# Sliding-window attention and a gated FFN on one core: loads ordered closer to the scores, early scores in separate banks, new engine orders

## The chip, the cores and the metric

The kernel runs on one core of a Trainium2 chip. The metric is the device time of one execution in microseconds, the median of several runs; less is better. A core has TensorE (matmul; the profile lists its weight loads as PEld), VectorE (DVE), ScalarE (ACT), GpSimd (POOL) and SyncE (SP). Each works through its own list of instructions in order. Here POOL and SP mostly issue DMA transfers, which 16 DMA engines carry out.

## The reference

Four sequences, eight heads, 768 positions, head dimension 64. Each query sees the last 128 positions and the four first ones (the sinks); the result goes through RMS normalisation and a gated FFN.

```python
scores = scale * np.matmul(q, k.transpose(0, 1, 3, 2))
keep = (pos[None, :] < 4) | ((rel >= 0) & (rel < 128))
a = softmax(np.where(keep, scores, -1e9))
x = np.matmul(a, v)                       # to [3072, 512]
xn = x / np.sqrt(np.mean(x * x, axis=-1, keepdims=True) + 1e-06) * rms_g
g = xn @ w_gate                           # 512 x 1536
out = (g * sigmoid(g) * (xn @ w_val)) @ w_out
```

## The kernel before

**Blocks.** The 3072 rows are 24 blocks g of 128 (six per sequence, or batch, b). In this text q5, k5, v5 are the loads of block 5, qT5 and kT5 the transposed tiles.

**Attention of a block.** POOL loads q, k and v, cast to bf16 by the DMA (L353, L357); block 0's q and k come through SP in float32 and are cast on an engine (L349). For blocks 0 to 7 q and k are transposed on TensorE (L445) and copied to the tile `qkT` by DVE or ACT (L452); from block 8 on SP does it with DMA transposes (L459). Scores are kept transposed: keys of block g against the queries of g (the own part) and of g+1 (the next part). Blocks 0 and 1 have their mask added by a matmul (L467) and no mask product. Blocks 2, 3, 6, 12 and 18 do whole scores (L485) and a mask product on DVE (L547); the others do only the needed triangles (L563, or L501 for the last of a batch), masked on DVE (L584) or from block 16 on POOL (L597, L526). ACT takes the exponentials (L536, L572, L512). AV (L616, L621) sums e times v, with a column of ones in the v tile giving the denominators. Those ones are written by DVE, one memset for each batch (L278). Sinks have their own small scores (L742), exponentials (L751) and AV (L606, L641); their v rows come by four SP loads into `vsink`, which DVE first clears (L326), and DVE makes `vsk` of them (L734). DVE divides (L660, L661), called n below; ACT squares (L669); DVE does the rest of the normalisation in eight small steps (L676 to L693), called the x chain. The gain `gb` is a product of TensorE, scaled by ACT (L428, L431). x is transposed on TensorE (L708) and copied (L714) for blocks 0 to 7, by SP's DMA transposes (L720) after that.

**FFN.** Six groups of four blocks. For a chunk of columns, g and v matmuls (L975), tanh on ACT (L982), two DVE steps (L988, L998), and the output matmuls (L1008), copied out by ACT (L1016) and stored by SP. Group 0 goes in four chunks of 128 columns, groups 1 and 2 in two of 256.

**Order.** Every step is entered with `op` in a fixed sequence, and so has a number. `ORDER` lists for each engine the numbers in the order in which the engine gets them, `TURNS` interleaves the engines, and `BANKS` gives each PSUM tile one of eight banks. What a step "needs" is only checked against these lists; the waits in the program come from the data: tiles read, written or reused, and banks taken again. `LOAD_LEAD`, `LEAD_FROM`, `GATE_FROM` and the priorities were used to make the lists and enter the program through them alone. Fifty-six small matmuls on zeros (`warm`, L421) stand in TensorE's list as fillers, all of them before 22 us.

A bank holds 512 float32 for each partition. The scores of a whole block take four, two heads with own and next part side by side in each:

```python
out=BANK[slot][:, j * 256 + n0 * P:j * 256 + n1 * P],
lhsT=qkT[pr, 1, hp, t * P:(t + 1) * P],
rhs=qkT[pr, 0, hp, (t + n0) * P:(t + n1) * P],
```

The first loads in POOL's list are q1, ident (make the identity), bias (make the mask), k1, v0, wg 0-1, q2, q3, v1, k2. In SP's list the stages of k0 and q0 come first, then the gain row and the sink rows.

Of the kernel before, what the change touches and what calls it, by code (L numbers as in the profile page):

```python
# [89 lines left out]
""",  # L90
    "ACT": """
24 20 22 199 177 175 178 176 182 180 181 183 168 188 222 204-206 211 207 212 209 191 210
217 226 228 227 229 195 598 220 236 603 613 618 608 243 633 628 260 623 245 247 246 248
638 278 262 255 264-267 197 280 282 284 653 273 320 648 643 295 297 659 290 322 299 301
300 302 276 324 325 293 326 327 309 664 678 669 683 674 333 312 693 340 316 341 688 342
343 698 355-357 336 358 703 370 371 708 372 318 373 349 385 364 387 718 713 723 739 379
399 401 400 402 728 418 419 733 420 393 421 409 763 758 778 768 754 773 744 749 427 433
414 783 434-436 448 449 793 450 798 451 442 808 788 819 803 463-466 813 457 824 480 475
482 494 496 497 495 513 488 514 515 504 834 838 516 848 843 853 829 863 868 858 878 873
525 883 531-533 893 509 888 534 899 923 549-551 928 552 938 543 567-569 918 570 585 587  # L100
933 943 948 561 953 579 958 909 904 968 593 963 914 973 1008 1003 994 998 1013 1028 1023
989 1038 1018 1033 984 1053 1048 1043 979 1069 1059 1064 1072 1073
""",
    "DVE": """
# [13 lines left out]
""",  # L118
    "POOL": """
25 8 9 26-28 31 34 30 32 37 35 29 38 33 39 41 42 40 43 45 47 44 48 46 49 36 50 53 57 52  # L120
54 51 56 63 62 60 55 58 64 61 59 65-99 467 469 468 470 481 100 483 101-108 517 520 109
518 519 535 538 537 536 110 553 555 554 571 573 556 572 588 586 574
""",
    "SP": """
# [7 lines left out]
ASDDSDGDPDPSPDPPPPPGPPPGPDPGPPDDPGAGPPPPADGPPPPGPPSPDPSADPGSDPSPGAAAPAGPAPPDAPPGPPAPDPAP  # L132
PPPADPGPDAGPPDPPDGAPPGPAPPAGDPAPAPDGADAPDGPAPPPADPAGPDAPADAGPPPPAPADGAPADGPPPPPAPPDPGPPD
DPAGPDPAGPDPGAPDDGPDGPDADGDPDGPADADPGAADPGPGDPADGAPDPGADAPGADADPGDPAPPDAPPDADAPGDPPADAGP
AAGPAPDAPPDPADPDAPGDAPDDGDPAPGDPPGSAAPGADAPGDPDGPPPDAGDAPGDADPPGADPAGDSAPPAGASPADPADSADP
PPGADAPGPSADDPGASAPGDPGSAPPGDPSADGAPDASDAPPDADPAGPPSAAADPAADPADPDAPAGADPGADPPDAPPADDPDGS
PDAPASAGDPPAPAGDSPADAPADDPPAGSADPPDASDPAGPADPSDDPGAPDDPADAPDGSDPDGPAGAPADSAPPADSDPPDGPDS
PDAGASPAAPDASGDPADSPDSDPGSPPPDDPSDGPDADPAPADPSDPSPDPSPDDAPDPDAPADPADAPDADAPDPDPASAPDASAP
DSADPADPDPASAPASADPAPPDASDPDAPSDASPADPDADPDPDPDAPASAPPDASADPAGPDGPGDPDGAPDPDPDPDAPAAGPSA
DGPAASGPADSPAGDPPGDDPGPPDGPDAAGPPDAGADPAGPAAGDPADAGPGPDSPGDPDASGPDGAADSPDAPDSDPPDSPDAPDS  # L140
ADPDSAPPDSDPSDAPDASPADDPDPDPADAPAAPDASADPADSPGSDGPDGSPGPGPAPAPADPAPDADPADAPDAGAPDGPGPAAP
AAPPADGDPPDGPDGDGPPAAPDSPGDPGAGPDAPPDPDPDPDAADPADPDDPAPAADPSDPDPDDPAAPPSPDDPAAPDPPSPPDPA
PSDSDSPASDPDPPPAAPDDPDPDPPAAPSDPDPAPDDPDPPPPAAPDADPSDPAAPDPDPAAPDDPDPDAPADPDPDPDPPDPAAPD
SPSDPPPPPAAPSASSPAADS
"""
BANKS = """
0123456701234567012345645645635654353513714370432704614654154761061305147237235720165760
7615743764051726351402376152376015237653746573746574631547613547647136210735462047136524
7012473650241762350741602735410721356421305406354063420675134632745013274350174362507431
6542371607152374153275461237104573604156324175032407615342047562310462317460170414217326  # L150
5047314243270172316412040572153042573045
# [4 lines left out]
def kernel(  # L156
# [40 lines left out]
    LOADS = "q-1 k-1 v-0 w-0-2 v-1 qkv-2 qkv-3 w-2-4 w-4-6 w-6-8 w-8-9 w-9-10 w-10-12 qkv-4 wo-0-6 qkv-5 wo-6-12 qkv-6 qkv-8 qkv-7"  # L197
    LOADS += "".join(f" qkv-{g}" for g in range(9, NB))
# [6 lines left out]
    GATE_FROM = 8  # L205
    LOAD_LEAD = 10
    LEAD_FROM = 10
# [146 lines left out]

    def load_v(g):
        b, t = divmod(g, NT)
        nc.gpsimd.dma_start(out=V16[b][:, t, :, 0:D], in_=block_of(v, g))  # L357
# [26 lines left out]
    def sw_block(g, what="qkv"):  # L384
        for n in what:
            needs = [("s", g - LOAD_LEAD)] if g >= LEAD_FROM else []
            if n == "v":
                sw_load(lambda g=g: load_v(g), [("v", g)], 860,
                        needs=needs + [("vone", g // NT)])
            else:  # L390
                src = q if n == "q" else k
# [57 lines left out]

    def copy_t(n, g, eng):  # L450
# [13 lines left out]
    def mask_bias(g):  # L464
        for u in range(2):
            for hi in range(2):
                nc.tensor.matmul(  # L467
                    out=bank(("s", g, u, hi)), lhsT=ident if g % NT else idnos,
                    rhs=bias.rearrange("p n c -> p (n c)").unsqueeze(1).to_broadcast(
                        (P, 2, 2 * P)),  # L470
                    start=True, stop=False, skip_group_check=True,
                )

    def scores(g, n0, n1):
        b, t = divmod(g, NT)
        qkT = T["qkT", b]
        for u in range(2):
            for j in range(2):
                hp = 2 * u + j
                for hi in range(2):  # L480
                    pr = slice(hi * D, (hi + 1) * D)
                    slot = ("s", g, u, hi)
                    if slot not in BANK:
                        bank(slot)
# [656 lines left out]
```

## Time and profile before

| | |
|---|---|
| median of 3 runs | 241.71 us (241.56 to 242.35) |
| span of the profiled execution | 241.9 us |
| TensorE / DVE / ACT / POOL busy | 231.3 / 187.4 / 122.8 / 89.2 us |
| FFN first stage on TensorE (L975) | 143.5 us |
| output matmuls (L1008) | 65.3 us |
| last matmul group's evacuation starts | 238.97 us |
| POOL loads q, k, v, 128 KB each | 8.1, 9.6, 8.9 us from issue to landing, median |
| DMA transposes to `qkT` | 7.7 (q) and 9.0 us (k) |

The page cuts the span into 40 slices of 6.05 us; a digit is the busy share in tenths. TensorE's busy time overlaps, since a matmul's latency counts though the next one has started; the distance from start to start is the better price. Lines of a timeline give the start, the time until the last of the merged instructions ends, engine, line, operation and tile, and in brackets the idle time before and what ended it. A chain of waits is followed back from the last instruction to what released it.

### The profile page before, as it was taken

The page shows a single profiled execution, that of the slowest core. Times are in us where ns is not written, and L with a number is a line of the kernel's source. Part 1 is how long each engine was busy: PE and PEld are TensorE (multiplying, and loading weights), DVE is VectorE, ACT ScalarE, POOL GpSimd, SP SyncE. Part 2 cuts the span into 40 slices and gives each one's busy share as a digit, 9 for nine tenths or more (in the row PEclk, how much of TensorE's full clock was granted, in tenths as well). Part 3 has the DMA queues.
Part 4 walks back from the last instruction along what each step waited for, and adds up shares of the span by engine and source line. Part 5 has one row for each costly group of instructions (what it writes and reads, how often), then busy time and mean ns, then how long its engine had stood idle before and what let it go on. Part 6 is the DMA issues. An engine that isn't in the chain of part 4 may idle for free.

```text
span 241.9 us, 5897 instructions
## 1 busy us (share of the span) xinstructions
PE 231.3 (96%) x2329; PEld 147.6 (61%) x2354; DVE 187.4 (77%) x478; ACT 122.8 (51%) x267; POOL 89.2 (37%) x116
## 2 busy tenths in 40 slices
PE   7889999999879999999999999999999999999995
PEld 5568986876668776777876644445554444444443
DVE  3599989989979999999898989994569946537520
ACT  4776368667766574337654464454543321233112
POOL 8985894597526554000004982022540000000000
PEclk9999999999999999999999999999999999999999
DMA  9999999999999999999601999527010114101024
GB/s 128 143 183 195 182 178 194 162 143 139 137 151 152 138 143 154 132 233 156 126 2 24 119 150 123 131 70 128 3 23 0 32 36 173 43 0 47 0 87 173
DMA packets 113741, 27.42 MB, mean 113 GB/s; under 512 B 103857, under 2 KB 110769, under 8 KB 113714
## 3 DMA queue, kind: packets, MB, share of 16 engines
q0 software_dynamic: 81760, 13.90, 79.3%
q1 hardware_dynamic: 31810, 12.95, 29.8%
q8 instruction: 18, 0.29, 0.5%
q10 hardware_dynamic: 144, 0.20, 0.2%
q14 instruction: 9, 0.07, 0.1%
HBM read 28.35 MB, written 6.29 MB: 143 GB/s over the span
## 4 chain that ended last, share of the span: by engine, by line
PE 67%; DMA 20%; POOL 6%; issue 2%; DVE 2%; SPq 2%; POOLq 0%
PE v L975 20%; PE o L1008 20%; PE g L975 18%; DMA wo<-in_moe_w_out_dram 5%; DMA qkT<-q 4%; DMA wv<-in_moe_w_val_dram 4%; DMA wg<-in_moe_w_gate_dram 3%; DMA q<-in_q_dram 3%; POOL v L357 2%; SPq L459 2%; PE s L563 2%; PE av L621 2%; POOL k L353 1%; PE av L616 1%; PE o_last L1028 1%
## 5 line engine op out<-in xcount | busy, mean ns | idle before, releaser
L975 PE MATMUL v<-xnt,wv 128*128 128x128 bf16 (+2 forms) x527 | 72.2, 282 | 0.4 <-DMA wv<-in_moe_w_val_dram 0.2
L975 PE MATMUL g<-xnt,wg 128*128 128x128 bf16 (+2 forms) x521 | 71.3, 281 | 0.4
L1008 PE MATMUL o<-wo,hT 128*128 128x512 bf16 x259 | 65.3, 379 | 1.1 <-issue 0.5
L982 ACT ACTIVATE th<-g 128x512 bf16<-128x512 f32 x72 | 41.7, 599 | 48.4 <-PE g L975 48.2
L988 DVE SCALAR_TENSOR_TENSOR p<-th,g 128x512 bf16<-128x512 bf16 x72 | 48.1, 682 | 18.9 <-ACT th L982 18.7
L975 PEld LDWEIGHTS <-wv 128*128 128x128 bf16 x528 | 43.3, 98 | 21.3 <-DMA wv<-in_moe_w_val_dram 0.6
L998 DVE TENSOR_TENSOR hT<-p,v 128x512 bf16<-128x512 bf16 x72 | 48.1, 682 | 9.3 <-PE v L975 7.8
L975 PEld LDWEIGHTS <-wg 128*128 128x128 bf16 x528 | 42.8, 98 | 19.3 <-issue 1.0
L1008 PEld LDWEIGHTS <-hT 128*128 128x128 bf16 x276 | 25.4, 98 | 26.5 <-issue 0.2
L597 POOL TENSOR_SCALAR_AFFINE_SELECT e<-e 128x512 bf16<-128x512 bf16 x20 | 12.7, 656 | 54.4 <-ACT e L572 53.0
L572 ACT ACTIVATE e<-s 128x384 bf16<-128x384 f32 x52 | 23.1, 495 | 12.5 <-PE s L563 12.5
L1016 ACT ACTIVATE osb<-o 128x512 f32<-128x512 f32 x23 | 13.4, 597 | 21.8 <-PE o L1008 18.0
L357 POOL DMA_DIRECT2D v<-in_v_dram x24 | 21.3, 888 | 8.5 <-DMA q<-in_q_dram 3.8
L353 POOL DMA_DIRECT2D q<-in_q_dram x23 | 20.4, 891 | 9.9 <-DMA k<-in_k_dram 6.7
L353 POOL DMA_DIRECT2D k<-in_k_dram x23 | 20.4, 889 | 9.1 <-DMA v<-in_v_dram 4.5
L669 ACT ACTIVATE sq<-x 128x512 bf16<-128x512 bf16 x24 | 15.1, 631 | 14.8 <-DVE x L661 14.5
L661 DVE TENSOR_TENSOR x<-av,rden 128x256 bf16<-128x256 f32 x48 | 20.4, 424 | 1.7
L693 DVE SCALAR_TENSOR_TENSOR xr<-x,r,gb 128x512 bf16<-128x512 bf16 x24 | 18.7, 778 | 0.8
L621 PE MATMUL av<-v,e 128*128 128x65 bf16 x192 | 16.4, 193 | 0.3 <-DMA v<-in_v_dram 0.3
L536 ACT ACTIVATE e<-s 128x512 bf16<-128x512 f32 (+1 forms) x36 | 15.1, 519 | 1.6 <-PE s L485 1.5
L616 PE MATMUL av<-v,e 128*128 128x65 bf16 x160 | 14.8, 193 | 0.0
L621 PEld LDWEIGHTS <-e 128*128 128x128 bf16 x192 | 12.7, 97 | 2.8 <-DVE e L547 0.4
(78 smaller groups left out, 192.6 us busy)
## 6 DMA issues: line engine op xcount, KB each, us to landing
out_dram<-osb SPq DMA_DIRECT2D x23, 256.0 KB, 2.2
v<-in_v_dram POOLq DMA_DIRECT2D x24, 128.0 KB, 8.9
q<-in_q_dram POOLq DMA_DIRECT2D x23, 128.0 KB, 8.1
k<-in_k_dram POOLq DMA_DIRECT2D x23, 128.0 KB, 9.6
wo<-in_moe_w_out_dram POOLq DMA_DIRECT2D x2, 768.0 KB, 11.3
wg<-in_moe_w_gate_dram POOLq DMA_DIRECT2D x5, 256.0 KB, 8.0
wv<-in_moe_w_val_dram POOLq DMA_DIRECT2D x5, 256.0 KB, 8.9
stage<-in_k_dram SPq DMA_DIRECT2D x1, 256.0 KB, 3.0
```

What stands on the lines that cost most here:

```text
L353: nc.gpsimd.dma_start(out=T[name, g], in_=block_of(src, g))
L357: nc.gpsimd.dma_start(out=V16[b][:, t, :, 0:D], in_=block_of(v, g))
L572: nc.scalar.activation(out=e_tile(g)[:, x:x + 2, 0:TW], in_=BANK.pop(("s", g, u, hi))[:, 0:2 * TW].rearrange("p (j c) -> p j c", c=TW), fu ...
L616: nc.tensor.matmul(out=dest, lhsT=T["e", g - 1][:, x, P:2 * P], rhs=V16[b][:, t - 1, h, :], start=(t == 1), stop=False, skip_group_check=True,
L621: nc.tensor.matmul(out=dest, lhsT=T["e", g][:, x, 0:P], rhs=V16[b][:, t, h, :], start=(t == 0), stop=True, skip_group_check=True,)
L661: nc.vector.tensor_tensor(out=T["x16", g][:, 4 * u:4 * u + 4, :], in0=pvv[:, :, 0:D], in1=rden.unsqueeze(2).to_broadcast((P, 4, D)), op=AL ...
L693: nc.vector.scalar_tensor_tensor(out=T["xr", g], in0=T.pop(("x16", g)).rearrange("p h d -> p (h d)"), scalar=r[:, 3:4], in1=gb, op0=ALU.mu ...
L975: nc.tensor.matmul(out=ps[:, i * n:(i + 1) * n], lhsT=w_sb[:, kt, ft * P:(ft + 1) * P], rhs=T["xnt", G][:, kt, cols], start=(kt == 0), sto ...
L982: nc.scalar.activation(out=T["th", key], in_=BANK[("g", key)], func=ACT.Tanh, scale=0.5,)
L988: nc.vector.scalar_tensor_tensor(out=T["p1", key], in0=T.pop(("th", key)), scalar=1.0, in1=BANK.pop(("g", key)), op0=ALU.add, op1=ALU.mult,)
L998: nc.vector.tensor_tensor(out=T[hk][:, i:i + n, cols], in0=T.pop(("p1", key)).rearrange("p (n c) -> p n c", n=n), in1=BANK.pop(("v", key)) ...
L1008: nc.tensor.matmul(out=BANK[("o", G, tb)], lhsT=T["h", G, ft // 4][:, ft % 4, tb * P:(tb + 1) * P], rhs=wo[:, ft, :], start=(ft == 0), sto ...
```

## The change

Three things. `LOAD_LEAD` and `LEAD_FROM` go from 10 and 10 to 6 and 8, and `GATE_FROM` from 8 to 24, so that no scores are gated; the load list is in order of blocks. Whole blocks' scores put the own part of four head pairs in one bank and the next part in another, so that each part has two banks of its own; matmuls become twice as many and half as wide outside blocks 0 and 1, the mask matmul goes by part, exponentials take 4 heads of one part (512 columns) instead of two heads with both, and in blocks 0 and 1 they are half as many. The lists of all engines, the turns and the banks are new. Code for loads of two blocks at once is added and unused (`PAIRS` is empty).

```diff
-    LOADS = "... wo-6-12 qkv-6 qkv-8 qkv-7"
-    LOADS += "".join(f" qkv-{g}" for g in range(9, NB))
+    PAIRS = ()
+    LOADS = "... wo-6-12 qkv-6 qkv-7"
+    LOADS += "".join(f" qkv-{g}" for g in range(8, NB))
...
-    GATE_FROM = 8
-    LOAD_LEAD = 10
-    LEAD_FROM = 10
+    GATE_FROM = NB
+    LOAD_LEAD = 6
+    LEAD_FROM = 8
...
+    def mask_bias(g, n):
+        for hi in range(2):
+            nc.tensor.matmul(
+                out=bank(("s", g, n, hi)), lhsT=ident if g % NT else idnos,
+                rhs=bias[:, n:n + 1, :].to_broadcast((P, HP, P)),
...
+    def scores(g, n):
+        for hp in range(HP):
+            for hi in range(2):
+                slot = ("s", g, n, hi)
...
+                    out=BANK[slot][:, hp * P:(hp + 1) * P],
+                    lhsT=qkT[pr, 1, hp, t * P:(t + 1) * P],
+                    rhs=qkT[pr, 0, hp, (t + n) * P:(t + n + 1) * P],
...
+    def exps(g, n, hi):
+        nc.scalar.activation(
+            out=e_tile(g)[:, hi * HP:(hi + 1) * HP, n * P:(n + 1) * P],
+            in_=BANK.pop(("s", g, n, hi)).rearrange("p (x c) -> p x c", c=P),
```

In words, the beginnings of the new lists (the numbers in `ORDER` read as steps; wN stands for N fillers):

```text
POOL  q2 ident k1 q3 v0 q1 bias k2 v1 q4 k3 wg4-5 wg0-1 wg2-3 v2 wg6-7 wv2-3 wv0-1 v3 ...
      q6 q7 wo0-5 wo6-11 k8 v6 q8 k7 v7 q9 q10 k9 v10 q11 k10 v8 ... q16 v19 k19 q20 v15 k16 ...
SP    k0 gain q0 sink rows qT8 kT8 qT9 qT10 kT9 qT11 ...
ACT   table q0 gb kT0 e0(own) x2 qT1 square0 e0 e1 e0 e1 e2 e1 e2 e2 e2 kT3 square1 sink e3 xT0 ...
PE    w27 kT0 w1 gain qT0 w2 qT2 w5 mask0 w3 s0(own) kT1 mask1 AV0 s1(next) AV0 w1 qT1 mask0 qT3
      s0(next) s1(own) kT2 w4 s2 w1 AV1 qT4 xT0 kT3 sink w2 s3 w1 g AV2 xT1 w1 g g w5 g v AV3 xT2 ...
DVE   ... n0 n0 masks qT3 ksk0 clear-vsink kT2 x0 e2 n1 qT4 n1 e2 vsk0 x1 n2 n2 e3 x2 ...
      h h h n4 p n5 ones(batch 1) n4 ...
```

In the list before, the memset of batch 1's ones stands fifth on DVE, and that of `vsink` ninth. Three fillers now stand behind the last matmul.

More of the change, by code (lines that the diff above doesn't have):

```diff
@@ L138 @@
[L138 to L143, printed above, removed]
@@ L152 @@
+7452745067534207564237536142561420376270127346516247353765026450243750624106752140673140
+5374610253704527132540736105476305476203172506325012453170453267410326702364701532457301
+4625460534715064715260472504261450261752607543207350467352046372154630457142052341064752
+4631075760564014076125047601726543607236
 """
@@ L353, in load_bf16, with load_pair @@
         nc.gpsimd.dma_start(out=T[name, g], in_=block_of(src, g))
+    def load_pair(name, src, g):
+        b, t = divmod(g, NT)
+        T[name, g] = ld.tile([P, H, 2, D], BF16, name=f"{name}2", bufs=2)
+        nc.gpsimd.dma_start(
+            out=T[name, g].rearrange("p h j d -> p h (j d)"),
+            in_=src[b, :, t * P:(t + 2) * P, :].rearrange("h (p j) d -> p h (j d)", j=2),
+        )
     def load_v(g):
@@ L448, in pe_t, with pe_pair, copy_pair @@
             )
+    def pe_pair(n, g):
+        ps = bank((n, g)).bitcast(BF16).rearrange("p (x c j) -> p x j c", x=HP, j=2)
+        src = T.pop((n, g))
+        for hp in range(HP):
+            for j in range(2):
+                nc.tensor.transpose(
+                    out=ps[:, hp, j, :], in_=src[:, 2 * hp:2 * hp + 2, j, :], identity=ident,
+                )
+    def copy_pair(n, g, i, eng):
+        b, t = divmod(g + i, NT)
+        ps = BANK[n, g].bitcast(BF16).rearrange("p (x c) -> p x c", x=HP)
+        eng(
+            out=qk_tile(b)[:, "qk".index(n), :, t * P:(t + 1) * P],
+            in_=ps[:, :, i * P:(i + 1) * P],
+        )
     def copy_t(n, g, eng):
@@ L462, in dma_t @@
         )
[L464 to L474, printed above, removed]
+    def mask_bias(g, n):
[3 more added lines that the diff above has]
+                rhs=bias[:, n:n + 1, :].to_broadcast((P, HP, P)),
+                start=True, stop=False, skip_group_check=True,
+            )
+    def scores(g, n):
         b, t = divmod(g, NT)
         qkT = T["qkT", b]
[L477 to L484, printed above, removed]
-                    nc.tensor.matmul(
-                        out=BANK[slot][:, j * 256 + n0 * P:j * 256 + n1 * P],
-                        lhsT=qkT[pr, 1, hp, t * P:(t + 1) * P],
-                        rhs=qkT[pr, 0, hp, (t + n0) * P:(t + n1) * P],
-                        start=g >= PE_MASKS, stop=True, skip_group_check=True,
-                    )
+        for hp in range(HP):
+            for hi in range(2):
+                pr = slice(hi * D, (hi + 1) * D)
+                slot = ("s", g, n, hi)
+                if slot not in BANK:
+                    bank(slot)
+                nc.tensor.matmul(
+                    out=BANK[slot][:, hp * P:(hp + 1) * P],
+                    lhsT=qkT[pr, 1, hp, t * P:(t + 1) * P],
+                    rhs=qkT[pr, 0, hp, (t + n) * P:(t + n + 1) * P],
+                    start=g >= PE_MASKS, stop=True, skip_group_check=True,
+                )
     def scores_last(g):
@@ L777, in block_scores @@
         b, t = divmod(g, NT)
-        nq = 2 if t + 1 < NT else 1
         pa = -1000.0 + 10 * g
         early = -20.0 + g if g < 2 * GB else 0.1 * g
-        slots = [("s", g, u, hi) for u in range(2) for hi in range(2)]
-        parts = [(0, 1), (1, 2)] if g in SPLIT else [(0, nq)]
+        slots = [[("s", g, n, hi) for hi in range(2)] for n in range(2)]
+        parts = [(0,), (1,)] if g in SPLIT else [(0, 1)]
         if g < PE_MASKS:
-            pe(864, lambda g=g: mask_bias(g), [("bias", 0), ("bias", 1), "ident", "idnos"]
-               + ([("qp", g), ("kp", g)] if g else []), [("mb", g)], pa, takes=slots)
-        for n0, n1 in parts:
-            needs = [("kT", g)] + [("qT", g + i) for i in range(n0, n1)] + gate_of(g)
-            needs += [("s", g - 1)] if g and not merged else []
-            needs += [("s", g, 0)] if n0 else []
-            needs += [("mb", g)] if g < PE_MASKS else []
-            last = (n0, n1) == parts[-1]
-            gives = [("s", g, n0)] + ([("s", g)] if last else [])
-            takes = slots if g >= PE_MASKS and n0 == 0 else []
-            ns, work = 220 * (n1 - n0), [lambda g=g, n=(n0, n1): scores(g, *n)]
+            for n in range(2):
+                pe(432, lambda g=g, n=n: mask_bias(g, n), [("bias", n), "ident", "idnos"],
+                   [("mb", g, n)], pa, takes=slots[n])
+        for ns_ in parts:
+            needs = [("kT", g)] + [("qT", g + n) for n in ns_] + gate_of(g)
+            needs += [("s", g - 1, 0)] if g and not merged else []
+            needs += [("mb", g, n) for n in ns_] if g < PE_MASKS else []
+            last = ns_[-1] == 1
+            gives = [("s", g, n) for n in ns_] + ([("s", g)] if last else [])
+            takes = [s for n in ns_ for s in slots[n]] if g >= PE_MASKS else []
+            ns, work = 220 * len(ns_), [lambda g=g, n=n: scores(g, n) for n in ns_]
             if last:
@@ L798, in block_scores @@
                 ns, work = ns + more, work + extra
-            if merged and n0 == 0:
+            if merged and ns_[0] == 0:
                 more, banks, given, other = merged
@@ L812, in block_scores @@
                         ns += 53 * n + 100
[L813 to L834 removed]
+            pe(ns, lambda work=work: [w() for w in work], needs, gives, pa + 1 + ns_[0],
+               takes=takes, mode=1)
+        for n in range(2):
+            for hi in range(2):
+                act(485, lambda g=g, n=n, hi=hi: exps(g, n, hi),
+                    [("s", g, n), "table"] + ([("av", g - 2, i) for i in range(2)] if g >= 2 else []),
+                    [("x", g, n, hi)], early, drops=[("s", g, n, hi)])
+        T["xs", g] = [("x", g, n, hi) for n in range(2) for hi in range(2)]
+        es = []
+        for n in range(2):
+            xs = [("x", g, n, hi) for hi in range(2)]
+            if g >= PE_MASKS:
+                dve(600, lambda g=g, n=n: mask_dve(g, n), xs + ["masks"], [("e", g, n)], early)
+                xs = [("e", g, n)]
+            es.append(xs)
+        T["es", g, 0] = T["es", g, 1] = es
     def tri_block(g):
@@ L882 @@
         for n in "qk":
-            if g < QK_DMA_FROM:
+            if g in PAIRS:
+                pe(446, lambda n=n, g=g: pe_pair(n, g), [(n, g), "ident"] + old, [(n + "p", g)],
+                   pa, takes=[(n, g)])
+                for i in range(2):
+                    ways = {"DVE": (345, lambda n=n, g=g, i=i: copy_pair(n, g, i, nc.vector.tensor_copy)),
+                            "ACT": (470, lambda n=n, g=g, i=i: copy_pair(n, g, i, nc.scalar.copy))}
+                    either(ways, [(n + "p", g), "table"] + ([(n + "T", g)] if i else []),
+                           [(n + "T", g + i)], early, drops=[(n, g)] if i else ())
+            elif g - 1 in PAIRS:
+                pass
+            elif g < QK_DMA_FROM:
                 pe(225, lambda n=n, g=g: pe_t(n, g), [(n, g), "ident"] + old, [(n + "p", g)],
```

95 lines of the change are left out of this document (33 added, 62 removed), and 76 rows, old and new, of the table ORDER.

## The prediction

> **What bounds the kernel now.** I read the page's busy table and slices first, then the first 50 us in order of time, then the chain of waits from 40 to 75 us, then the v loads by their line.
>
> ```profile
> PE 231.3 (96%) x2329; PEld 147.6 (61%) x2354; DVE 187.4 (77%) x478; ACT 122.8 (51%) x267; POOL 89.2 (37%) x116
> ...
> PE   7889999999879999999999999999999999999995
> PEld 5568986876668776777876644445554444444443
> DVE  3599989989979999999898989994569946537520
> ...
> PEclk9999999999999999999999999999999999999999
> ```
>
> TensorE is the bound from 20 us on; it loses time at the start and in slice 11 (60 to 70 us). DVE is nearly as full up to slice 26, so a late DVE is soon a late TensorE.
>
> I measure lost time as **lag**: when an operation starts on TensorE, less the TensorE work ordered ahead of it, fillers not counted. Prices are start-to-start intervals: a transpose of four pieces 0.22 us, a mask matmul 0.216, scores of one block 0.44 (two halves of 0.22), a group of sixteen 128-column FFN matmuls 0.896, the gain product 0.94, AV of a block without sink 0.48. Ahead of block 2's x transpose stand ten transposes (2.25), eight mask matmuls (1.73), the gain (0.94), three blocks' scores (1.32), three AVs (0.26 + 0.48 + 0.71), a sink score (0.12) and six FFN groups (5.38): 13.19. It starts at 24.59, so the lag is 11.40.
>
> ```profile
> 3.55 2.66 SPq L329 DMA_DIRECT2D vsink<-in_v_dram  x4
> 5.42 1.79 POOL L353 DMA_DIRECT2D q<-in_q_dram  x2
> 10.80 0.70 DVE L734 TENSOR_TENSOR vsk<-vsink,headm 128x520 bf16<-128x520 f32 x1 [0.38 <-DMA vsink<-in_v_dram]
> 11.42 0.40 PE L445 MATMUL q<-ident,q 128*128 128x128 bf16 x4 [0.38 <-DMA q<-in_q_dram]
> ...
> 14.80 0.58 ACT L714 COPY xnt<-x 128x512 bf16<-128x512 bf16 x1
> ...
> 16.06 0.61 PE L485 MATMUL s<-qkT 64*128 64x256 bf16 x8
> 16.60 1.07 PE L975 MATMUL g<-xnt,wg 128*128 128x128 bf16 x16
> 17.17 2.04 ACT L536 ACTIVATE e<-s 128x512 bf16<-128x512 f32 x4
> ```
>
> Here the first FFN group starts at 16.60, after ACT's copy of the first x tile at 14.80; ACT's long run for block 2 comes behind that copy. The fifth POOL load takes 6.0 us from issue to use, the sink rows 4.5 from their last issue.
>
> ```profile
> 32.09 12.88 DMA wo<-in_moe_w_out_dram
> ...
> 45.26 0.87 POOL v L357
> ...
> 47.27 7.30 DMA q<-in_q_dram
> ...
> 54.59 1.20 SPq L459
> ...
> 59.75 10.61 DMA qkT<-q
> ...
> 70.49 0.54 PE s L563 x16
> ```
>
> The loss in slice 11: block 9's q is issued behind the second wo load, four DMA transposes follow one another on SP, and block 9's scores wait. By the same count the lag is 13.9 at block 5's x transpose (56.60, 42.71 ahead) and 16.58 at these scores (70.49, 53.91 ahead): 2.7 us.
>
> **The change part by part.** The work is the same but for small pieces. I read the two orders off the numbers in the tables.
>
> *Load lead and gate.* Both only restrain the order; the program has no wait of a load for scores, nor of scores for an FFN step. What holds a load back is the landing of the one eight before it on POOL (v of block 6 leaves POOL at 45.26, wo's landing at 44.97 released it). So this part moves loads, and saves or costs nothing by itself.
>
> *The head.* POOL now opens q2, ident, k1, q3, v0, q1 and only then the bias: at 0.89 a load the bias is made at about 6.5 instead of 2.66. SP sends the gain ahead of q0's stage, so q0 is cast on ACT at 5.3 instead of 4.75; DVE casts k0 (not shown; between the 0.42 of its bf16 copy and ACT's 0.62, hidden by q0; without that cover 0.2). First scores at about 7.8 instead of 6.39. q1 is the fifth load instead of the first: issued at 5.33, used at about 11.0, and its copy is third from the front of ACT's queue, so square 0 and all later exponentials wait for it until 11.7. Then ACT must do square 0 (0.73), nine exponentials (0.51 each, from the 2.04 for four), k3's copy, square 1 (held until about 18.4 by DVE, which has the x chain of block 0, 2.0 us, two n's, a mask and two copies before it), the sink's exponential and one more exponential, and only then copies x tile 0: 20.5 instead of 14.80. The old order ran sixteen exponentials of 0.29 for blocks 0 and 1 where the new one runs eight of 0.51; these 0.56 us of ACT are in the chain.
> DVE clears the sink tile after block 0's n's, at 13.3 instead of 3.24. The four sink loads wait for that on SP, and so land at 13.3 + 2.7 + 4.5 = 20.5; behind them on DVE stands block 1's x chain, so its transpose comes at 23.2. Four FFN groups later (one behind a filler run, 0.3) the first v group starts at 26.5. Ahead of it stand eleven transposes (2.48), masks 1.73, gain 0.94, four blocks' scores 1.76, AVs 1.45, sink 0.12, four FFN groups 3.58: 12.07. Lag 14.45: **3.05 more than before.** Bounds: 1.0 if q1 and the sink rows land at the quickest landing in the trace (2.5 from issue), 5 if they take the 8.9 us of its usual v load. I take the rows of the same stage.
>
> *Separate banks.* Blocks 2, 3, 6, 12 and 18 now do sixteen matmuls of 128 columns with sixteen weight loads instead of eight of 256. Eight of 128 take 0.33 start to start (12.49 to 12.82), eight of 256 0.54 (16.06 to 16.60): 5 x (0.66 - 0.54) = **0.6**. Bounds: 0, as in the triangle scores, where 24 short ones take 0.47; 3.8 if none of 40 loads of 0.094 hid behind another. [...]
>
> *v loads behind a memset.* The first v load of each later batch has its own semaphore wait:
>
> ```profile
> L357 POOLq EVENT_SEMAPHORE  x3: 17/17/17, 33.7 to 86.9; - x3
> ```
>
> These fall just ahead of v8, v12 and v18, the first of their batches: they wait for DVE's ones in the v tile. Before, DVE set these long ago. Now batch 1's memset stands behind block 5's first n: from block 2's x chain, done at 27.4, DVE has 17 FFN steps of 0.605, four n's of 0.57, an x chain and 2.7 us of masks ahead, so about 45. v6 is held from 37 to 45 and behind it every load: q8, k7, v7, q9 (issued at 48.8), q10, k9 (50.6). At the 7.3 us of the chain above q9 lands at 56.1; its transpose, now third on SP after kT8, at 10.6 is through by 66.7. The other estimate, by transfer (wo's second half three loads later, q9 six loads after it, 0.96 each from the ten loads between 44.97 and 54.57), gives 53.6 and 64.2. TensorE reaches block 8's scores at 49.42 + 14.45 + 2.5 (before's growth from 11.4 to 13.9) = 66.4, and block 9's at 70.9, whose k9 is through by 69. **So the 2.7 us wait is gone**, because TensorE is late itself: lag 17.0 against 16.58. Bounds: none of it saved, or all and up to 1 more.
> Batch 3's memset comes at about 91, so POOL stands still from 81; v15 and k16 behind it still land by 105, and are needed from 120.
>
> *Later orders.* q21 and q22 are issued after a block 19 mask on POOL (before: ahead of it), and kT20 stands seventh on SP behind them: 8.5 us from block 19's scores to q22's issue, about 5 to land, 7 x 1.26, 2.4: 24.7 against 24 us of TensorE work. Between 0 and 2 us; I take 0, as it is the nearer end. Tail and fillers after the last matmul: 0, behind the last store.
>
> **Sum.** 241.88 + 3.05 - 2.7 + 0.6 = 242.8 in the profiled execution's terms; that one is 0.17 over the median of 241.71. Predicted: **242.7**, slightly slower.
>
> **Rivals.**
> 1. *Faster: more attention done early.* By 20.5 us the new order has four blocks' scores and nine transposes behind it and DVE's later peaks are lower. If x tile 0 is copied by 18.5 rather than 20.5, everything behind is 2 us earlier, the memset too, and slice 11's wait still goes: 240.7. It decides from a head lag under 13.1. For: the old head also idled on ACT and DVE. Against: ACT's queue. Chance 0.28.
> 2. *Memset late.* If DVE reaches it at 48 or later, q9's transpose and block 8's scores slip with it, 1 for 1: 245. For: DVE 9 tenths full there. Against: the transfers before it last until 46 anyway. 0.16.
> 3. *kT20 late*: 2 us, 244.7. 0.08.
> 4. *The clock drops in the head.* The first mask matmuls took 541 ns against 377 for the later four, though the clock row says full; TensorE now idles up to 2 us at a time near 19 us. [...] 0.04. [...]
>
> The forecast holds 0.44.
>
> **How the numbers follow.** Under 0.3% (0.73 us) cannot be told from no change here. The forecast of 242.7 lies 1.0 above the old median; about a quarter of its 0.44 falls within 0.73, a quarter of rival 1 too: same 0.19; the rest of rival 1 and a little of the forecast: faster 0.25; slower 0.56. The range takes rival 1 with 1.5 us more out of the head (239.2), and upward the forecast with the head at its upper bound (+1.95) and the whole of rival 3 (246.6).
>
> **What would show it.** Right: the first FFN group near 20.5, the sink product on DVE idle for its load until about 20, POOL standing at v6 until DVE's memset near 45, no wait of TensorE near 65 to 71, sixteen score matmuls at 0.66. Wrong: the first FFN group by 18.5, or block 8's scores starting after 68.

## The result and the profile after

The changed kernel takes 249.79 us (median of 4 runs, 247.52 to 250.38) against 241.87 us before (4 runs, 241.56 to 242.35): ratio 1.0306, 95% interval 1.0259 to 1.0353. It is slower, 7 us above the 242.7 predicted and outside the range. The profiled execution has a span of 245.8 us; it is the run of 247.52, its shortest, so the span lies 1.7 below the device time. Times, ratios and comparisons here and below leave out slow runs, those over 1.5% above the fastest of the same kernel: one each of tail_back and fill_gaps, two of head_po, three of inputs_early, with the profiled executions of fill_gaps and inputs_early among them.

The busy table and slices of the page after (slices of 6.15 us):

```profile
PE 234.9 (96%) x2394; PEld 150.6 (61%) x2394; DVE 187.6 (76%) x479; ACT 121.2 (49%) x258; POOL 90.6 (37%) x116
...
PE   7886999999999999999999799999999999999994
...
PEclk9797999999999999999999999999999999999999
```

The dent in slice 11 is gone. In its place TensorE is emptier in slices 4 and 23, and the clock row, full before, has two dents in the head. The head in order of time:

```profile
6.65 0.62 ACT L350 CAST q<-stage 128x512 bf16<-128x512 f32 x1 [4.57 <-DMA stage<-in_q_dram]
...
9.58 0.61 PE L513 MATMUL s<-qkT 64*128 64x128 bf16 x8
...
15.06 0.28 DVE L327 MEMSET vsink<- 128x260 f32 x1
...
15.37 2.67 SPq L330 DMA_DIRECT2D vsink<-in_v_dram  x4
...
21.35 0.58 ACT L734 COPY xnt<-x 128x512 bf16<-128x512 bf16 x1
...
21.98 1.87 PE L998 MATMUL g<-xnt,wg 128*128 128x128 bf16 x16 [1.77 <-ACT xnt L734]
...
22.45 0.70 DVE L754 TENSOR_TENSOR vsk<-vsink,headm 128x520 bf16<-128x520 f32 x1 [1.91 <-DMA vsink<-in_v_dram]
...
25.18 0.41 PE L728 MATMUL x<-ident,xr 128*128 128x128 bf16 x4
...
25.70 1.95 PE L998 MATMUL g<-xnt,wg 128*128 128x128 bf16 x32
...
29.95 0.39 PE L728 MATMUL x<-ident,xr 128*128 128x128 bf16 x4
```

This is the chain of the prediction, each link later than forecast: q0 cast at 6.65 (5.3), first scores 9.58 (7.8), sink tile cleared 15.06 (13.3), sink rows in use 22.45 (20.5), first FFN group 21.98 (20.5). Block 2's x transpose starts at 29.95 with the 13.31 us of work of the new order ahead of it: lag 16.64, against 14.45 predicted for the head and 11.40 before.

The same stretch cut where TensorE's speed changes (columns: stretch, its length, busy time and instructions of each engine, granted clock, DMA share, GB/s):

```profile
0.00:8.50 8.50, 5.88 (x50) 4.52 (x51) 2.13 (x10) 2.87 (x4) 7.30 (x14) 0.98 1.20 117
8.50:12.00 3.50, 3.50 (x24) 1.80 (x23) 0.85 (x3) 1.08 (x2) 3.50 (x5) 0.56 2.40 153
12.00:22.00 10.00, 7.07 (x121) 4.73 (x120) 7.62 (x27) 8.19 (x19) 8.45 (x11) 0.99 1.62 183
22.00:25.50 3.50, 3.48 (x39) 3.19 (x39) 2.84 (x10) 1.52 (x3) 2.35 (x3) 0.54 1.88 177
```

Read in windows of 0.02 us, the granted clock is 0.50 from 8.17 to 11.58 and from 21.82 to 25.23, twice 3.41 us. Each stretch comes with a TensorE wait: the first begins 0.85 us after the end of one of 1.35 us for q0 (up to 7.32), the second in the last 0.16 us of one of 1.77 us for the first FFN group (up to 21.98). Later, one wait remains:

```profile
48.35 0.87 POOL L366 DMA_DIRECT2D v<-in_v_dram  x1 [11.15 <-DVE rden L680]
...
138.87 0.54 PE L583 MATMUL s<-qkT 64*64 64x192 bf16 x24
141.11 1.24 PE L998 MATMUL g<-xnt,wg 128*128 128x512 bf16 x5 [1.70 <-DVE m L696]
...
242.04 0.49 ACT L1066 ACTIVATE last<-o_last 128x384 f32<-128x384 f32 x1 [1.30 <-PE o_last L1051]
```

POOL does stand 11 us at v6; block 8's and 9's scores nevertheless start at 67.38 and 72.14 without a wait. Group 3's first g matmul waits 1.70 us, for block 15's x tile, whose DMA transpose lands at 140.98. And the last evacuation is now the 384-column piece on ACT: from its start to the end of the span 3.76 us (245.8 - 242.04), before 2.9 (241.9 - 238.97).

### The profile page after: what moved, and what is told of

Same layout as the page of the kernel before. It is cut to its first block, busy times and chain, and to the rows that moved or that the text cites. A ratio compares the mean times of both kernels' runs of the same rounds, so it can differ in the third digit from the quotient of the medians.

```text
span 245.8 us, 5993 instructions
## 1 busy us (share of the span) xinstructions
PE 234.9 (96%) x2394; PEld 150.6 (61%) x2394; DVE 187.6 (76%) x479; ACT 121.2 (49%) x258; POOL 90.6 (37%) x116
## 4 chain that ended last, share of the span: by engine, by line
PE 86%; DMA 5%; POOL 5%; DVE 2%; ACT 0%; issue 0%
PE v L998 26%; PE g L998 26%; PE o L1031 24%; DMA wv<-in_moe_w_val_dram 4%; PE s L583 2%; PE av L641 2%; PE av L636 2%; POOL v L366 1%; POOL wg L414 1%; DMA stage<-in_k_dram 1%; PE o_last L1051 1%; POOL q L354 1%; POOL k L354 1%; PE s L513 1%; POOL wv L414 1%; PE x L728 1%
## 5 line engine op out<-in xcount | busy, mean ns | idle before, releaser
L998 PE MATMUL g<-xnt,wg 128*128 128x128 bf16 (+2 forms) x528 | 72.2, 285 | 3.5 <-ACT xnt L734 1.8
L998 PE MATMUL v<-xnt,wv 128*128 128x128 bf16 (+2 forms) x528 | 71.4, 282 | 0.0
L1031 PE MATMUL o<-wo,hT 128*128 128x512 bf16 x276 | 67.8, 379 | 0.0
L998 PEld LDWEIGHTS <-wg 128*128 128x128 bf16 x528 | 43.7, 99 | 23.2 <-issue 3.9
L617 POOL TENSOR_SCALAR_AFFINE_SELECT e<-e 128x512 bf16<-128x512 bf16 x20 | 13.8, 716 | 52.3 <-ACT e L592 48.7
L354 POOL DMA_DIRECT2D q<-in_q_dram x23 | 20.9, 916 | 2.7 <-DMA v<-in_v_dram 0.8
L641 PE MATMUL av<-v,e 128*128 128x65 bf16 x192 | 17.2, 195 | 0.0
L560 ACT ACTIVATE e<-s 128x512 bf16<-128x512 f32 x28 | 14.9, 609 | 4.4 <-PE s L513 2.5
L641 PEld LDWEIGHTS <-e 128*128 128x128 bf16 x192 | 13.4, 99 | 3.0 <-ACT e L560 0.2
L636 PE MATMUL av<-v,e 128*128 128x65 bf16 x160 | 14.9, 196 | 0.1
```

Source lines behind the costliest of these rows:

```text
L354: nc.gpsimd.dma_start(out=T[name, g], in_=block_of(src, g))
L636: nc.tensor.matmul(out=dest, lhsT=T["e", g - 1][:, x, P:2 * P], rhs=V16[b][:, t - 1, h, :], start=(t == 1), stop=False, skip_group_check=True,
L641: nc.tensor.matmul(out=dest, lhsT=T["e", g][:, x, 0:P], rhs=V16[b][:, t, h, :], start=(t == 0), stop=True, skip_group_check=True,)
L998: nc.tensor.matmul(out=ps[:, i * n:(i + 1) * n], lhsT=w_sb[:, kt, ft * P:(ft + 1) * P], rhs=T["xnt", G][:, kt, cols], start=(kt == 0), sto ...
L1031: nc.tensor.matmul(out=BANK[("o", G, tb)], lhsT=T["h", G, ft // 4][:, ft % 4, tb * P:(tb + 1) * P], rhs=wo[:, ft, :], start=(ft == 0), sto ...
```

## The experiments

All times are medians in us with lowest, highest and number of runs; ratios are to runs of the kernel before on the same chip (medians 241.72, 241.91, 241.88, 241.98). Order edits are shown as pieces of the lists, in the names used above.

| kernel | time | ratio, 95% interval |
|---|---|---|
| ones_early | 249.78 (248.57-250.71, 4) | 1.0316 (1.0268-1.0364) |
| fill_gaps | 248.77 (247.85-250.41, 3) | 1.0288 (1.0234-1.0343) |
| copy_early | 249.54 (249.29-250.91, 4) | 1.0322 (1.0287-1.0357) |
| tail_back | 248.70 (246.78-249.28, 3) | 1.0235 (1.0167-1.0302) |
| q0_early | 248.50 (247.15-249.50, 4) | 1.0265 (1.0211-1.0318) |
| sink_early | 247.59 (246.35-248.30, 4) | 1.0233 (1.0191-1.0276) |
| sink_copy | 245.71 (245.07-245.98, 4) | 1.0152 (1.0122-1.0183) |
| inputs_early | 244.68 (243.39-245.37, 5) | 1.0108 (1.0074-1.0142) |
| head_nofill | 245.02 (244.32-245.50, 4) | 1.0127 (1.0095-1.0160) |
| head_all | 244.08 (243.34-245.08, 4) | 1.0087 (1.0053-1.0122) |
| head_po | 242.77 (242.20-245.70, 8) | 1.0064 (1.0025-1.0102) |
| gain_first | 243.04 (241.77-244.06, 10) | 1.0035 (1.0011-1.0059) |
| before_halves | 241.98 (241.52-242.21, 10) | 0.9996 (0.9979-1.0014) |
| before_q9 | 241.33 (240.72-242.08, 10) | 0.9979 (0.9963-0.9995) |

**The held loads.** ones_early:

```diff
 DVE list
- ... n5 ones(batch 1) n4 ...   ... ones(batch 3) ...
+ id bias zeros ones(batch 0) ones(batch 1) ones(batch 3) k0 ...
```

> The changed kernel with the memsets of the ones of batches 1 and 3 moved to the start of DVE's list, so that no v load waits for them. Theory A: TensorE did not wait for these loads (it is full from 30 to 130 us in the profile of the change), so the time stays within 1 us of 249.8. Theory B: POOL no longer stands for 11 and 17 us, and the time falls by 3 us or more, to 247 or less.

249.78 against 249.79, with nearly the same interval: POOL's waits of 11 and 17 us cost nothing that shows. DVE's late memset is no cause.

**Half-width scores in the kernel before.** before_halves:

```diff
-    nc.tensor.matmul(out=BANK[slot][:, j*256+n0*P : j*256+n1*P], ...
-        rhs=qkT[pr, 0, hp, (t+n0)*P : (t+n1)*P], ...)
+    for n in range(n0, n1):
+        nc.tensor.matmul(out=BANK[slot][:, j*256+n*P : j*256+(n+1)*P], ...
+            rhs=qkT[pr, 0, hp, (t+n)*P : (t+n+1)*P], ...)
```

> The kernel before with the scores of blocks 2, 3, 6, 12 and 18 as sixteen matmuls of 128 columns instead of eight of 256, in the same banks. The prediction's price: 5 x 0.12, so 0.6 us more than before. [...]

No difference: 0.6 us would be a ratio of 1.0025, and the interval ends at 1.0014. The 40 more weight loads cost nothing that shows, and the term of 0.6 was wrong: sixteen matmuls take 0.56 us from start to start here (16.08 to 16.64) and 0.55 in the changed kernel (block 6, 49.29 to 49.84), where eight of 256 took 0.54. There neighbours change between the two halves of the partitions; in before_halves the two matmuls of a pair follow each other on the same half, and take no more than 0.02 above the 0.54 either. Its profile, span 240.4, also shows what the kernel before usually does at block 9's scores: start 69.02, lag 15.11, where the execution behind the prediction had 70.49 and 16.58.

**The inputs of the head.** inputs_early:

```diff
 SP list
-k0 gain q0 sink rows ...
+k0 q0 gain sink rows ...
 DVE list
-id bias zeros ...  qT3 ksk0 clear-vsink kT2 ...
+id bias zeros clear-vsink ...  qT3 ksk0 kT2 ...
 POOL list
-q2 ident k1 q3 v0 q1 bias k2 ...
+q2 ident bias k1 q3 v0 q1 k2 ...
```

> The changed kernel with three input steps moved back to the front and nothing else: SP sends block 0's q stage ahead of the gain row, DVE clears the sink tile at the start, POOL makes the mask right after the identity. Theory A (the loss is made in the head, by late inputs and ACT's queue, and by half-clock windows that its gaps bring on): q0 is cast near 5 us instead of 6.65, the sink product does not wait, the first FFN group starts 1.5 to 2.5 us earlier than 21.98, and the time falls from 249.8 to 245.5 to 248. Theory B (the loss is made by the loads held behind the late memsets of the ones, 11 and 17 us on POOL): the head moves, but the time stays within 1 us of 249.8.

Its median is 5.1 below the changed kernel's. These three steps of the head hold most of the loss.

**Tail.** tail_back:

```diff
 end of the lists
-last128 last384 ... fillers, ACT's evacuation and store last
+last384 last128 ... as in the kernel before
```

> The changed kernel with its last steps in the order of the kernel before: the 384 last columns, then the 128, which DVE copies out. From the profiles (3.8 us from the last copy's start to the end against 2.9) both theories expect 0.9 us less, 248.9.

1.1 less by the medians, but the intervals overlap: in agreement with the 0.85 read off the trace, not shown by the times.

**Which part of the head?** fill_gaps fills the waits ahead of block 0's q transpose and of the first FFN group, copy_early takes away the cause of the second.

```diff
 fill_gaps
-        nc.tensor.matmul(out=ps[:, 0:P], lhsT=zeros, rhs=zeros, ...)
+        for _ in range({12: 20, 20: 28}.get(i, 1)):
+            nc.tensor.matmul(out=ps[:, 0:P], lhsT=zeros, rhs=zeros, ...)
 copy_early, ACT list
-... kT3 square1 sink e3 xT0 e1 ...
+... kT3 xT0 square1 sink e3 e1 ...
```

> The changed kernel, with 19 more filler matmuls in the wait ahead of block 0's q transpose (6.0 to 7.3 us) and 27 more ahead of the first FFN group (20.2 to 22.0 us). Nothing else moves; the fillers end before the data arrives. Theory C (the two windows of half TensorE clock, 8.5 to 12 and 22 to 25.5 us, come from those two waits and are most of what the head lost beyond the late inputs): mean granted clock 0.998 or more in most runs, lag at block 2's x transpose 13.5 to 15.0 instead of 16.64, median 246.3 to 248.3 us. Theory A alone (only the inputs' lateness counts, the clock is a by-product): lag within 0.4 of 16.6, median 249.3 to 250.3.

> The changed kernel, with ACT's copy of the first x tile put straight behind k3's copy, ahead of square 1, the sink's exponential and one exponential of block 3 (its x transpose is done at 18.2, ACT copies it at 21.35). Theory A' (ACT's order holds the first FFN group): that group starts at 20.0 to 20.5 instead of 21.98, the wait of 1.77 us is below 0.5, and with it the second window of half clock goes in most runs: median 246.5 to 248.5 us. Rival (what holds the head is the sink rows at 22.45 and all that DVE has behind them; the group only runs earlier and TensorE waits later): median 249.2 to 250.3, lag at block 2's x transpose within 0.5 of 16.64.

Neither shows a gain: 248.77 and 249.54, with intervals that overlap that of the changed kernel; fill_gaps lies between its two theories. In copy_early the group ran at 20.77 without a wait, and TensorE stopped right behind it. Its timeline:

```profile
20.77 1.05 PE L998 MATMUL g<-xnt,wg 128*128 128x128 bf16 x16
...
23.91 0.27 PE L626 MATMUL av<-vsk,esk 128*128 128x260 bf16 x1 [2.09 <-DVE m L696]
...
25.89 0.61 PE L728 MATMUL x<-ident,xr 128*128 128x128 bf16 x4 [1.10 <-DVE xr L713]
```

The matmul at 23.91 takes `vsk`, so it waits for the sink rows; block 1's x transpose then waits for the x chain that stands behind the `vsk` product on DVE. So in this trace the sink rows hold the head just behind the copy. TensorE ran at a granted clock of 0.50 from 25.30, within the second of these waits, to 32.13 (mean of this execution 0.979), and block 2's x transpose started at 33.46: a lag of 20.15, not the 16.64 of the rival, though the time is the rival's. sink_early clears the sink tile at the start of DVE's list and changes nothing else, sink_copy has this and copy_early's edit:

```diff
 DVE list
-id bias zeros ...  qT3 ksk0 clear-vsink kT2 ...
+id bias zeros clear-vsink ...  qT3 ksk0 kT2 ...
```

> The changed kernel, with the sink tile cleared at the start of DVE's list, nothing else. Its four loads then leave SP right behind q0's stage and land near 10 us. Theory T (two limits of nearly the same lateness stand side by side in the head: ACT's copy of the first x tile, 21.35, holds the first FFN group; the sink rows at 22.45, behind them block 1's x chain on DVE, hold block 2's AV and the second x tile): without the sink rows the copy alone still holds the group at about 21.9, so at most 1.0 us is won: 248.7 to 250 us. Rival (the sink rows are the one limit, as the prediction's head was worked out): block 1's x transpose 2 us earlier and with it all behind: 246.5 to 248.2.

> The changed kernel, with both the sink tile cleared at the start and the first x tile copied straight behind k3's copy. Theory T: neither edit alone is worth 1 us (copy_early was 249.54), both together let the first FFN group start at 20.3 to 20.9 and block 1's x transpose at 22.5 to 23.5, with no wait of over 1 us there: 246.0 to 248.0 us. Rival (q0's lateness and the half-clock window at 8.5 to 12 us are what counts, and both remain): 248.7 to 250.

By the medians the sink rows alone are worth 2.2 us (249.79 to 247.59), which is what the rival of theory T gave; but the intervals overlap a little (1.0191 to 1.0276, 1.0259 to 1.0353), and the trace of sink_early shows theory T:

```profile
20.67 0.69 DVE L754 TENSOR_TENSOR vsk<-vsink,headm 128x520 bf16<-128x520 f32 x1
...
22.19 1.87 PE L998 MATMUL g<-xnt,wg 128*128 128x128 bf16 x16 [1.77 <-ACT xnt L734]
...
25.18 0.57 PE L728 MATMUL x<-ident,xr 128*128 128x128 bf16 x4
```

The rows are there, yet the first FFN group still waits 1.77 us for ACT's copy and takes 1.87 us as in the changed kernel (1.05 in copy_early), and block 1's x transpose starts at 25.18 in both. Copy and rows are two limits of nearly the same lateness. What the 2.2 us between the medians consist of is not shown. Both edits together are worth 4.1 us (249.79 to 245.71), and the second of them 1.9 (247.59 to 245.71), each with intervals apart; the copy alone is worth nothing by the medians (249.54).

**q0 and the bias.** gain_first does one part in the kernel before, q0_early undoes it in the changed one (with the bias):

```diff
 gain_first, SP list
-k0 q0 gain sink rows ...
+k0 gain q0 sink rows ...
 q0_early: SP list k0 q0 gain ...; POOL list q2 ident bias k1 ...
```

> The kernel before, with one part of the change alone: SP sends the gain row ahead of q0's stage. The prediction's price: q0 cast 0.55 us later, all of it on the path: 242.2 to 242.5. What the changed kernel's trace suggests (stage issued behind a 1 us issue, landing 1.9 us later): q0 cast at about 6.5, first scores at 8.0 to 8.3 instead of 6.39, and 1.2 to 1.9 us later at the end: 242.9 to 243.8. Rival (the early exponentials have slack, or the block 9 wait swallows it): within 0.3 of 241.8.

> The changed kernel, with q0's stage sent ahead of the gain row and the bias made behind the identity; the sink tile is still cleared where the changed kernel clears it, behind block 0's divisions. Theory (the sink rows are the one limit of the head, sink_early won 2.2, and q0 only shifts the moment of their clearing): the divisions and with them the clearing and the rows come 1 to 1.7 us earlier, and the end by as much: 248.1 to 248.9. Rival 1 (q0 is worth its 1.1 us of gain_first and the clock's half windows besides): 246.5 to 248. Rival 2 (the clearing is held by DVE's other work): 249.3 to 250.

One place in SP's list costs the kernel before 1.1 us by the medians; the ratio of 1.0035 (1.0011 to 1.0059) means 0.3 to 1.4 us, which holds the 0.55 of the prediction too. Undone together with the bias, the changed kernel's median is 1.3 lower, but the intervals overlap, and the trace of q0_early does not show the earlier divisions of its theory: q0 was cast at 4.80, but TensorE was at half speed from the start (gain product 2.07 us, 1.12 in the changed kernel; see below), the sink tile was cleared at 16.57 instead of 15.06, and block 1's x transpose started at 26.88 instead of 25.18. The stage left SP at 1.31 before and at 1.83 after, but was cast 1.9 us later (4.75 and 6.65). Other traces agree: cast at 4.70 to 5.58 in seven with q0 first, at 6.51 to 6.93 in seven with the gain first.

**Half clock.** head_all is inputs_early with the early copy, the old tail and 18 more fillers (8 and 12 in the places of fill_gaps' 20 and 28); head_nofill is the same without those fillers.

```diff
 head_all against head_nofill
-            nc.tensor.matmul(out=ps[:, 0:P], lhsT=zeros, rhs=zeros, ...)
+        for _ in range({12: 8, 20: 12}.get(i, 1)):
+            nc.tensor.matmul(out=ps[:, 0:P], lhsT=zeros, rhs=zeros, ...)
```

> The changed kernel with everything found so far put right: q0's stage ahead of the gain row, sink tile cleared at the start, bias made behind the identity (as in inputs_early, 245.25), the first x tile's copy early, 7 and 11 extra fillers in the two waits, and the last steps in the old order. Theory: the head's inputs, ACT's order, the clock and the tail are the whole difference, so what is left over the kernel before is the 1.5 us of the later orders less the 1.3 us that the wait at block 9 costs it: 241.3 to 243.3 us. Rival (the gains are one and the same stretch of the head, only the tail's 0.85 adds to inputs_early): 244.2 to 245.2.

> The kernel head_all (244.08) without its 18 extra fillers; everything else as there. In sink_copy, which also lacks them, the gain product took 2.07 us and block 1's four mask matmuls 1.91, against 1.12 and 1.03 in head_all: TensorE ran at half speed until 13 us, though the clock row says full. Theory C (the waits of 1 to 2 us in the head bring half speed, and half speed in the head is lost time): gain product at 2.07 or mask matmuls at 1.9 in the profile, block 2's x transpose 0.8 to 2 us later than 26.14, median 244.9 to 246.2. Rival (half speed falls into time in which TensorE waits for other engines anyway): 243.7 to 244.5.

244.08 with the fillers, above the 243.3 that its theory allowed and just below its rival; 245.02 without. The intervals of the ratios overlap a little; the traces show where the time goes. head_nofill, then head_all:

```profile
4.83 2.07 PE L443 MATMUL gb<-grow,ones 1*128 1x512 f32 x2
...
8.44 1.02 PE L498 MATMUL s<-bias,idnos 128*128 128x512 bf16 x2
...
9.72 0.61 PE L513 MATMUL s<-qkT 64*128 64x128 bf16 x8
...
27.50 0.39 PE L728 MATMUL x<-ident,xr 128*128 128x128 bf16 x4
```

```profile
5.81 1.12 PE L444 MATMUL gb<-grow,ones 1*128 1x512 f32 x2
...
7.86 0.59 PE L499 MATMUL s<-bias,idnos 128*128 128x512 bf16 x2
...
8.55 0.40 PE L514 MATMUL s<-qkT 64*128 64x128 bf16 x8
...
26.14 0.39 PE L729 MATMUL x<-ident,xr 128*128 128x128 bf16 x4
```

The first q transpose starts at the same time in both (6.83 and 6.87). From there to block 0's scores it takes 2.89 us at half speed and 1.68 at full; at block 2's x transpose the distance is 1.36. So half speed in the head is lost time: 1.36 us by the traces, about 1 by the medians (245.02 - 244.08). The clock row of both pages is full throughout: head_nofill's half speed does not show there, only in the durations (gain product 2.07 us against 1.12).

Missing fillers alone do not bring it. Of eight traces of the changed order without extra fillers four ran the gain product at half speed (2.07 us in head_nofill, sink_copy and q0_early) and four at full (1.12 in the changed kernel's); head_all and head_po, with them, ran it at full. The trace of tail_back, whose head has the same order as the changed kernel's, is one of the first four. Later its granted clock is 0.50 from 23.56 to 30.38 (mean of this execution 0.986), twice as long as either stretch of the changed kernel's profiled run:

```profile
25.10 0.61 PE L728 MATMUL x<-ident,xr 128*128 128x128 bf16 x4 [0.84 <-DVE xr L713]
...
25.87 3.57 PE L998 MATMUL g<-xnt,wg 128*128 128x128 bf16 x32
...
32.21 0.39 PE L728 MATMUL x<-ident,xr 128*128 128x128 bf16 x4
```

Block 1's x transpose is as early as in the changed kernel (25.18), block 2's 2.26 us later than there (29.95), with the two FFN groups between at 3.57 us instead of 1.95. So these two heads of one order differ by 2.26 us there, 1.62 of it in the two groups at half clock. What decides the clock was not found.

**The later wait.** head_po is head_all with the last output matmuls of group 2 moved ahead of group 3's first g:

```diff
 PE list
-... scores19 g(group 3) g o(group 2) g ...
+... scores19 o(group 2) g(group 3) g g ...
```

> The kernel head_all (244.08), with the last output matmul of group 2 that follows the first FFN group of group 3 put ahead of it, where TensorE waits 1.1 to 1.9 us in every run of the changed kernel's orders (141.11, group 3's first g, for the x tile of block 15). Theory (that wait is lost time and the matmul fills it): the wait falls by 0.6 to 0.9 us, 243.2 to 243.6. Rival (block 15's chain on DVE and ACT sets what follows, the matmul only changes places): 243.9 to 244.4.

1.3 less by the medians, but the intervals overlap; the trace shows 1.2:

```profile
135.68 1.04 PE L1032 MATMUL o<-wo,hT 128*128 128x512 bf16 x4
137.17 2.75 PE L999 MATMUL g<-xnt,wg 128*128 128x512 bf16 x12 [0.46 <-DMA xnt<-xr]
```

The wait of 1.68 us of head_all is 0.46 here. The lowest run, 242.20, lies within the range of the kernel before; what spreads its runs up to 245.70 was not found.

**A version slightly ahead of both.** before_q9 aims at the one thing in which the change helped, no wait at block 9, by moving two loads and nothing else:

```diff
 POOL list of the kernel before
-... wo6-11 q7 v8 q8 v5 k6 k7 k8 v6 v7 q9 k9 ...
+... wo6-11 q7 q9 q8 v5 k6 k7 k8 v6 v7 v8 k9 ...
```

> The kernel before, with q9's load on POOL brought forward by eight loads, to just behind q7 (ahead of q8), and v8's put back behind v7. The one part of the prediction's gain that the changed kernel kept is that TensorE no longer waits at block 9's scores. Theory (the wait for qT9 is real and worth 0.5 to 1.3 us in the kernel before): 240.6 to 241.3, faster than both. Rival (DVE is as late there, or the next tile is): 241.6 to 242.0, no change; if q8's transposes slip, up to 242.6.

0.55 us faster than the kernel before by the medians, interval 0.9963 to 0.9995: small, and just clear of no change. Block 9's scores start at 67.67, without a wait.

## Why the prediction was wrong

The lag of each trace at three places (the start on TensorE less the work ordered ahead in that kernel):

| trace | block 2's x transpose | block 9's scores | block 20's scores |
|---|---|---|---|
| before, as predicted from | 11.40 | 16.58 | 19.39 |
| before_halves | 11.43 | 15.11 | 17.95 |
| before_q9 | 11.98 | 13.76 | 16.58 |
| after | 16.64 | 18.21 | 22.46 |
| tail_back | 18.90 | 20.47 | 24.83 |
| sink_early | 16.80 | 18.38 | 23.41 |
| sink_copy | 15.94 | 17.51 | 21.20 |
| head_nofill | 14.19 | 15.76 | 20.98 |
| head_all | 12.83 | 14.39 | 19.26 |
| head_po | 12.65 | 14.21 | 17.77 |

The profiled run of after is its shortest (247.52) and that of sink_early its longest (248.30). Their mean granted clock is the same, 0.986.

1. *The head, +3.05: right chain, wrong size.* It was +5.24 (16.64 - 11.40), above its upper bound of 5. The step that failed is "SP sends the gain ahead of q0's stage, so q0 is cast on ACT at 5.3": it was 6.65, 1.35 of the 2.2 missing. Another 0.43 came between cast and first scores (2.93 us instead of 2.5), with the masks there at half speed (the two at 8.32 in 1.01 us, the two at 12.88 in 0.59). From then on the chain kept the predicted distances: 1.76 late at the clearing, 1.95 at the sink rows, 1.98 at block 1's x transpose (25.18 for 23.2). The times show rows and copy together (4.1 us) and the copy once the rows are there (1.9); that the rows alone (2.2) or q0 with the bias (1.3) win time is not shown clear of noise, and not by their traces. The gain's place is shown in the kernel before (1.1).
2. *The clock, rival 4 with a chance of 0.04: it happened.* "TensorE now idles up to 2 us at a time" was right. The changed kernel's profiled run had two stretches of 3.41 us at half clock, tail_back one of 6.82 besides its half-speed start, and fillers won back about 1 us by the medians (245.02 - 244.08). What failed is the low chance: half clock came with waits of 1.35 and 1.77 us. The 0.04 was the author's estimate; no trace before the forecast had shown which waits bring half clock, or for how long.
3. *Slice 11, -2.7: the wait went, but it was not worth that.* It went because TensorE was late itself, as predicted. The size was read from one execution in which the wait was longer than usual: the lag grew 2.7 there from block 5's x transpose to block 9's scores and 1.0 in before_halves (14.09 to 15.11); mending it in the kernel before won 0.55.
4. *The base, "that one is 0.17 over the median".* Here a span was set against a device time. Device time less span is 1.7 to 1.9 in every run (247.52 and 245.8; 242.14 and 240.4), so the execution with the span of 241.9 was one of about 243.6, 1.9 above the median. With point 3 this is one error: the profiled execution was longer than usual, and 1.5 of its excess stood at block 9 (16.58 - 15.11).
5. *Separate banks, +0.6: 0.* The lower bound held.
6. *Memset and held loads: right.* The stop at v6 came (until 48.35, not 45), and rival 2, which priced a memset after 48 at 245, fell: ones_early.
7. *Later orders, 0: wrong place.* kT20 was not late (rival 3). Instead group 3's first g waited 1.70 for block 15's x tile, which the prediction does not mention; in head_po's trace 1.2 of that wait is gone.
8. *Tail, 0: 0.85 by the trace*, with the wide piece last.
9. *Rival 1, faster: fell.* It needed the first x tile copied by 18.5; the copy came at 21.35, and by copy_early an early copy alone would not have helped.

The traces add up. Against before_halves, whose run of 242.14 is an ordinary one of the old order, the changed kernel's lag is 5.2 more at block 2's x transpose, 3.1 at block 9's scores and 4.5 at block 20's; with 0.85 for the tail that is the 5.4 between the spans (245.8 and 240.4). The medians lie 7.9 apart, since the changed kernel's median run is 2.3 longer than the profiled one. In tail_back two FFN groups at half clock took 1.62 longer (3.57 and 1.95); that half clock made the 2.3 here was not shown. head_po won back 7.0 of the 7.9 (249.79 - 242.77). In its profiled run (242.23) nothing is left: its head is 1.2 later than the old one (12.65 and 11.43), but at block 20's scores its lag is the old one (17.77 and 17.95). Why its median is still 0.9 above stays open.

## What to carry to other kernels

Compare spans with spans: a wait seen in one profiled execution, in a span that stands high among its siblings, can promise more than its removal wins. In a start-up, follow the smallest late input (here a 256 KB stage one place back in a queue and a memset behind other work) through every engine to the last consumer; where two limits are nearly equally late, mend both before judging either. Look for half speed in the durations of matmuls of known shape, not in the clock row alone: here a gain product took 2.07 us instead of 1.12 under a full row. With the late inputs mended, fillers in the places of the two waits won about 1 us here by the medians (245.02 to 244.08); without that, nothing that shows (249.79 to 248.77).

## What the runs showed of the hardware

- In the changed kernel's trace the granted clock was 0.50 from 8.17 to 11.58 and from 21.82 to 25.23, 3.41 us each, next to the ends of waits of 1.35 us (up to 7.32) and 1.77 us (up to 21.98). The first FFN group took 1.66 us from start to start (21.98 to 23.64), one at full clock 0.89 (27.81 to 28.70). In copy_early, with waits of 2.09 and 1.10 us, it was 0.50 for 6.83 us; in tail_back, with a wait of 0.84 us (up to 25.10), for 6.82.
- The mean granted clock read 1.00 where the gain product took 2.07 us instead of 1.12 (head_nofill).
- SP's issue half a microsecond later (1.83 for 1.31) became a cast 1.9 us later: the stage, behind the gain row, took 4.8 us from issue to landing (to 6.63) instead of 3.4 (to 4.73).
